# Top-k attention followed by an FNet block on one core: another order for seven matrix products over two PSUM banks, and another bank for the tail transposes of q and k

## The chip, the cores and the metric

The kernel runs on one core of a Trainium2 chip. The core has a matrix engine (TensorE, PE in the profile, with PEld for its weight loads), a vector engine (VectorE, DVE), a scalar engine (ScalarE, ACT), a general engine (GpSimd, POOL) and a queue engine (SyncE, SP) that here only issues transfers. Each engine works through its own list of instructions in order; semaphores hold an instruction until what it needs has been done on another engine. The metric is the device time of one execution in microseconds (us), lower is better. Everything is computed in float32.

## The reference, cut to what matters

```python
# q, k, v: (8 batches, 8 heads, 576 tokens, 64)
scores = q @ k.T / 8                                # per batch and head: 576 x 576
kth    = 32nd largest of each row                   # top_k = 32
scores = where(scores >= kth, scores, -1e9)
attn   = softmax(scores)
x      = attn @ v                                   # heads joined: (8, 576, 512)

mixed  = real(fft(fft(x, axis=tokens), axis=channels))
u      = x + mixed
un     = (u - mean(u)) / sqrt(var(u) + 1e-6)        # over the 512 channels
out    = u + relu(un @ w_ch1) @ w_ch2               # 512 -> 2048 -> 512
```

So every batch goes through attention with a top-k mask, through a Fourier transform over tokens and channels, and through a two-layer network (MLP).

## The kernel before, in words

**Attention.** The 64 heads are taken as 32 pairs. A pair has nine tiles of 128 query rows, four for each head and one that holds the 64 last rows of both. That gives 288 tiles, and the main loop takes one step for each, 36 steps for a batch. For a tile, `scores` (L355) multiplies on PE into PSUM and ACT copies the result to SBUF (`S`, L396 to L425); `top_ops` (L428) finds the 32nd largest by four rounds of MAX8 (L446) and MATCH_REPLACE8 (L448) on DVE; `bounds` (L451) makes the threshold on POOL; `mask` (L466) takes an ACT pass (L469) and a POOL pass (L472); `expo` (L476) is the exponential on ACT (L480); `plane` (L487) splits the result in two 16-bit halves on ACT (L493), which SP stores and transposes by DMA; some tiles are transposed on PE instead. `attend` (L576) multiplies by v on PE (L585), `attended` (L594) copies on ACT, and `to_tokens` (L615) transposes back on PE (`tpx`, L626) for DVE to normalise into x (L630).

`prep` (L309) transposes q and k of the next pair. It does so in two blocks for each of them: the four full 128-row blocks together (columns up to `NF` = 4), and then the tail block. For q the tail block is read from `qtail` and turned by a matrix of `turns` (L329), and ACT copies the result to qT (L337); for k, ACT copies the full blocks to kT (L339) and the tail in two pieces to `kt_t` (L343). `prep("q", pair + 1)` is issued at the first step of each pair (i % 9 = 0), right behind that step's scores, `prep("k", ...)` at the sixth.

**Fourier transform.** For a batch that is complete, folds of x (L671 to L770, on POOL, for the last batch on DVE) use the symmetry of the transform, then PE multiplies by the token tables (`yp`, L809) and the channel tables (`mp`, L860, L864), POOL adds the result to x (L898), DVE takes the statistics, and PE transposes to channels-first (`tpu`, L948).

**MLP.** `mlp_units` (L1041) puts the MLP of a batch into a queue of small units of PE work, in two halves of tokens: `ch` 0 with token tiles 0, 1 and the tail tile 4, `ch` 1 with tiles 2 and 3. `hidden` makes 16 blocks of the first layer (`hp`, L1055, read by ACT at L1059). The second layer is either `back` (`cp`, L1082 and L1120), or, for two token tiles at a time, `fast` (L1155): a Strassen-like scheme in which seven products of half size take the place of eight. It is used for `ch` 0 from the second batch on and for `ch` 1 of the last two batches, nine times in all. The units are handed out one after another by the main loop, a certain amount of PE time for each step (`some`, `level`), so that the MLP of one batch runs between the attention steps of the next. Other work has fixed places in this plan, given by `at(step, place, function)`.

**The seven products.** Each product (L1254) has two parts of eight matmuls 128x256, which are two units. The result goes to half of a PSUM bank, called `v`, `w` and, in the last batch, `z`; where a later product adds to what lies there, the bank keeps it in place:

| product | bank, half | weights | then |
|---|---|---|---|
| p2 | v lo | w2_21 | ACT reads it to a buffer `ct` (L1225), an adder adds that to x (L1227) |
| p5 | v hi | `w2_12` (T1) | the same; issues the load of T2 into `w2_12` |
| p1 | w lo | w2 itself | the same; half sums "11" and "12" (L1198) |
| p4 | w hi (z hi in the last batch) | `second` (T4) | the same; issues the load of T3; half sum "22" |
| p6 | w lo | `w2_12` (T2) | the same; issues the load of B12 |
| p3 | v hi | w2 itself | DVE adds the half bank to one half of x (L1211), v comes free |
| p7 | w lo | `second` (T3) | DVE adds the half bank to both halves of x (L1211), w comes free |

Products that add to what is in a half bank come after ACT has read it. The half sums of hidden values ("21", then "11", "12", "22") are made by POOL, after the last attention step by DVE; "11" is needed by p6, "12" by p3, "22" by p7, "21" by p5. In the last batch all seven results go to x by DVE (L1211), without the buffer. With p3 and p7 the finished token tiles are stored (`store_rows`, L1023): tiles 0 and 2 by a plain transfer from SP (L1028), the others by an indirect one from POOL (L1031).

**PSUM.** There are eight banks: two for scores (`ps_s`, tag "sp"), two for transposes (`ps_t`, tag "tp"), one for attention outputs, and three common ones that `bank()` (L144) hands out in turn. A caller that passes `hold=True` takes a bank out of the turn until it gives it back: `fast` does so with v, w and z, `back` with `cp`. All others (`hp` and most of the Fourier products) take the next one in the turn. In `tp` buffers there are q's and k's transposes (`tpq`, `tpk`), the transposed score tiles of `scores` (`sp_t`) and the other transposes.

```python
banks_free = [0, 1, 2]
def bank(shape, name, hold=False):
    n = banks_free.pop(0)
    t = ps_m.tile(shape, F32, name=name, tag=f"m{n}", bufs=1)
    if not hold:
        banks_free.append(n)
        return t
    return t, lambda: banks_free.append(n)
```

Of the kernel before, what the change touches and what calls it, by code (L numbers as in the profile page):

```python
# [9 lines left out]
F32 = mybir.dt.float32  # L10
# [9 lines left out]
P = 128  # L20
# [66 lines left out]
def kernel(  # L87
# [16 lines left out]
    NF = NC - 1  # L104
# [4 lines left out]
    NPB = H // 2  # L109
# [26 lines left out]
    ps_t = ctx.enter_context(tc.tile_pool(name="ps_t", bufs=2, space=bass.MemoryType.PSUM))  # L136
# [7 lines left out]
# [7 lines that stand above are left out]
# [158 lines left out]
    def prep(n, pair, blocks=((0, NF), (NF, NC))):  # L309

        if pair >= NPAIR:
            return 0.0
        src, got_of = nat[n, pair], qT_of if n == "q" else kT_of
        if pair not in got_of:
            got_of[pair] = attp.tile(
                [P, S if n == "q" else NF * P], F32, name=f"{n}T_{pair}", tag=f"{n}T",
                bufs=2 if n == "q" else 1
            )
        t_sb = got_of[pair]
        for c0, c1 in blocks:  # L320
            tp = ps_t.tile([P, 4, P], F32, name=f"tp{n}_{pair}_{c0}", tag="tp")
            for c in range(c0, c1):
                block, turn_by = src[:, c, :, :], ident
                if n == "q":
                    turn_by = turns[:, 2 if c == NF else c % 2, :]
                    if c == NF:
                        hp = pair % NPB
                        block = qtail[:, 2 * hp:2 * hp + 2, :]
                nc.tensor.transpose(  # L329
                    tp[:, c - c0, :], block.rearrange("p h d -> p (h d)"), turn_by  # L330
                )
            if c0 < NF:
                dst, got = t_sb[:, c0 * P:c1 * P], tp.rearrange("p a c -> p (a c)")[:, 0:(c1 - c0) * P]
            else:
                dst, got = t_sb[:, NF * P:], tp[:, 0, 0:TAIL]
            if n == "q":
                nc.scalar.mul(out=dst, in_=got, mul=scale)  # L337
            elif c0 < NF:
                nc.scalar.copy(out=dst, in_=got)  # L339
            else:  # L340
                for e in range(2):
                    r = slice(D * e, D * (e + 1))
                    nc.scalar.copy(out=kt_t[r, TAIL * e:TAIL * (e + 1)], in_=tp[r, 0, 0:TAIL])  # L343
        return 0.7
# [696 lines left out]
    def mlp_units(b):  # L1041
        x = x_of[b]
        last = b == B - 1
# [111 lines left out]
        def fast(ch):  # L1155
# [164 lines left out]
            def begin():  # L1320
# [6 lines left out]
                (0.0, lambda: mix("21", "21", "22", ALU.add), "back")  # L1327
            ] + [
                (1.75, lambda f=f, part=part: f(part), "back")
                for f in (p2, p5, p1, p4, p6, *((p7, p3) if last and ch else (p3, p7)))  # L1330
                for part in range(2)
            ]

# [1 line left out]
        for ch in range(2):  # L1335
            units += [
                (8 * CW[ch] / 1200.0, lambda ch=ch, it=it: hidden(ch, it), ("hidden", b, ch))
                for it in range(NIT)
            ]
            seven = b and ch == 0 or b >= B - 2  # L1340
            if seven:
                begin, products = fast(ch)
                if ch == 0:
                    begins.append(begin)
                else:
                    units.insert(1 - NIT, (0.0, begin, ("hidden", b, 1)))
                mix_first = products.pop(0)
                units.append(mix_first)
            for t in [t for t in CHUNKS[ch] if t == 4 or not seven]:
                units += [  # L1350
                    (1.75, lambda ch=ch, t=t, p=p: back(ch, t, p), "back")
                    for p in range(4 if t == 4 else 8)
                ]
            if seven:
                units += products
# [28 lines left out]
    for t in v_t:  # L1384
        nc.gpsimd.memset(t[TAIL:P, 0, NF, :], 0.0)
        nc.gpsimd.memset(t[0:TAIL, 1, NF, :], 0.0)
    nc.gpsimd.memset(ftail, 0.0)
    prep("q", 0, ((0, 2),))
    prep("k", 0)
    for c in range(2):  # L1390
        scores(0, c)
    prep("q", 0, ((2, NF), (NF, NC)))
    scores(2, 0)

# [88 lines left out]
    for b in range(B):  # L1483
        end = PER_BATCH * (b + 1) - 1
        last = b == B - 1
# [54 lines left out]
    def chunk_at(i):  # L1540

        for tile in (i - 5, i - 4, i - 3, i - 2):
            r = tile % PER_PAIR
            if PER_BATCH <= tile < N and r in (4, 8):
                if i - tile == ((5 if r == 4 else 4) if by_dma(tile) else 2 if tile in (2 * PER_BATCH - 1, N - 1) else 3):
                    return tile // PER_PAIR, r // 8
        return None, None
# [41 lines left out]
    while i < N + 5 or plan or queue or sums:  # L1589
# [37 lines left out]
        if pending and pending[0][0] <= i and (  # L1627
            i < 2 * PER_BATCH + 4 or chunk_at(i)[0] is None
        ):
            _, pp, pc = pending[0]  # L1630
# [12 lines left out]
        if short:  # L1643
            fixed += tok
            pair, r = divmod(i - 1, PER_PAIR)
# [40 lines left out]
        pair, ch = chunk_at(i)  # L1686
# [81 lines left out]
```

## Time and profile before

| | |
|---|---|
| median of 3 runs | 1778.69 us (1776.69 to 1779.95) |
| the profiled execution | 1780.27 us, its span 1778.5 us |
| busy in the span: PE, DVE, ACT, POOL | 1632.1, 1552.5, 1278.8, 906.6 us |
| mean granted clock of PE | 0.964 |
| chain that ended last, by engine | PE 48%, DVE 16%, ACT 16%, POOL 14%, issue 5%, DMA 2% |
| the products, L1254 (`cw`) | 512 matmuls, 383 ns each; idle before them 9.1 us, 6.2 of it to ACT's read L1225 |
| the products, L1254 (`cv`) | 432 matmuls, 383 ns each; idle before them 6.6 us |
| `hp`, L1055 | 2048 matmuls, 409 ns each; idle before them 6.8 us |
| q's tail transposes (`tpq` from `qtail`) | 32, 9.9 us with 273 ns as the median; idle before them 9.5 us, 9.2 of it to ACT's copy L396 |

The span is the time from the first to the last instruction in the profile. "Busy" is time in which an engine works on something; "idle before" is the time in which the engine stood just before an instruction of that group, with the event that ended it. PE is not busy for some 146 us of the span, and much of that lies in the first two batches, where weights are loaded and converted: in the page's forty slices PE has 5 to 7 tenths in the first five, and 8 or 9 in nearly all that follow. DVE has 9 tenths from the start to about 1600 us and little behind that, when the attention is finished and only the last MLPs remain.

### The profile page before, as it was taken

To read this page: it belongs to the slowest core of one execution; us is meant where nothing else is said; L and a number is where in the kernel's file an instruction comes from. 1 tells how busy PE (TensorE), PEld (TensorE's weight loads), DVE (VectorE), ACT (ScalarE), POOL (GpSimd) and SP (SyncE) were. 2 spreads that over 40 slices of the span, in tenths; PEclk is the share of its full clock that TensorE was granted. 3 is DMA by queue.
4 is the path that set the end of the run, shared out by engine and by line. 5 is a ranking of instruction groups with operands and counts; after the bars stand their busy time and mean duration, and the time that the engine had idled before them with its cause. 6 is when DMAs were issued, how large, how long until landed. Compare 5 with 4: busy or idle time off the path is not lost.

```text
span 1778.5 us, 26295 instructions
## 1 busy us (share of the span) xinstructions
PE 1632.1 (92%) x7830; PEld 1040.9 (59%) x7830; DVE 1552.5 (87%) x3319; ACT 1278.8 (72%) x3136; POOL 906.6 (51%) x1268
## 2 busy tenths in 40 slices
PE   5666689999898989999999999999999999999998
PEld 3444455464455755566555755576566755577777
DVE  7999989999999999998999999999999999863121
ACT  6888759887787878876888778877978787653200
POOL 4768846655634565354544665356535564333000
PEclk7778799999999999999999999999999999999999
DMA  5333126651457855586557856595558655643151
GB/s 156 115 102 117 32 81 163 185 152 50 119 145 196 222 131 135 136 233 161 135 136 200 212 133 140 152 240 145 152 132 222 182 135 128 172 114 101 36 180 60
DMA packets 492926, 255.28 MB, mean 144 GB/s; under 512 B 364528, under 2 KB 483056, under 8 KB 492784
## 3 DMA queue, kind: packets, MB, share of 16 engines
q1 hardware_dynamic: 489008, 243.80, 52.5%
q0 software_dynamic: 2816, 9.44, 1.6%
q8 instruction: 63, 1.03, 0.2%
q14 instruction: 79, 0.65, 0.1%
q10 hardware_dynamic: 960, 0.36, 0.1%
HBM read 99.79 MB, written 84.74 MB: 104 GB/s over the span
## 4 chain that ended last, share of the span: by engine, by line
PE 48%; DVE 16%; ACT 16%; POOL 14%; issue 5%; DMA 2%; POOLq 0%; SPq 0%; DVEq 0%; ACTq 0%
PE hp L1055 18%; DVE m L446 7%; DVE wk L448 6%; PE o L585 6%; PE cw L1254 5%; POOL wk L472 5%; PE cv L1254 4%; PE sp L422 4%; ACT wk L469 3%; POOL fold L696 3%; PE cp L1120 2%; ACT wk L493 2%; PE cp L1082 2%; ACT S L425 2%; PE sp_t L392 1%
## 5 line engine op out<-in xcount | busy, mean ns | idle before, releaser
L472 POOL TENSOR_TENSOR wk<-S,wk 128x576 f32<-128x576 f32 x288 | 407.6, 1415 | 418.1 <-ACT wk L469 417.2
L446 DVE MAX8 m<-wk 128x8 f32<-128x576 f32 x864 | 617.4, 741 | 0.1
L1055 PE MATMUL hp<-unT,w 128*128 128x256 f32 (+1 forms) x2048 | 529.6, 409 | 6.8 <-ACT hT L1059 6.0
L1055 PEld LDWEIGHTS hp<-unT,w 128*128 128x128 f32 x2048 | 378.0, 191 | 112.0 <-ACT hT L1059 11.4
L448 DVE MATCH_REPLACE8 wk<-m,wk 128x576 f32<-128x576 f32 x576 | 424.8, 737 | 0.0
L469 ACT ACTIVATE wk<-S,nt 128x576 f32<-128x576 f32 x288 | 224.3, 779 | 96.8 <-POOL nt L455 96.3
L493 ACT COPY wk<-S 128x576 uint16<-128x576 uint16 x468 | 290.2, 673 | 0.0
L446 DVE MAX8 m<-S 128x8 f32<-128x576 f32 x288 | 214.5, 745 | 11.6 <-ACT S L396 11.6
L480 ACT ACTIVATE S<-wk,nt 128x576 f32<-128x576 f32 x234 | 185.1, 791 | 46.7 <-POOL wk L472 45.4
L448 DVE MATCH_REPLACE8 wk<-m,S 128x576 f32<-128x576 f32 x288 | 212.5, 738 | 0.0
L1082 PE MATMUL cp<-w,hT 128*128 128x512 f32 x448 | 206.0, 598 | 0.0
L1059 ACT ACTIVATE hT<-hp 128x320 f32<-128x320 f32 (+1 forms) x256 | 104.1, 411 | 140.7 <-PE hp L1055 139.7
L585 PE MATMUL o<-PT,v 128*64 128x256 f32 (+3 forms) x1440 | 196.1, 417 | 5.6 <-DVE wk L448 2.1
L422 PE MATMUL sp<-kT,qT 64*128 64x512 f32 (+1 forms) x528 | 160.1, 668 | 6.7 <-ACT S L414 3.6
L585 PEld LDWEIGHTS o<-PT,v 128*64 128x64 f32 x1440 | 113.2, 154 | 84.1 <-issue 24.8
L425 ACT COPY S<-sp 128x512 f32<-128x512 f32 (+1 forms) x264 | 141.7, 589 | 26.2 <-PE sp L422 25.2
L455 POOL TENSOR_TENSOR nt<-m,cc 128x2 f32<-128x2 f32 x288 | 58.7, 204 | 166.9 <-DVE m L446 160.4
L1254 PE MATMUL cw<-w,hT 128*128 128x256 f32 x512 | 119.7, 383 | 9.1 <-ACT ct L1225 6.2
L1082 PEld LDWEIGHTS cp<-w,hT 128*128 128x128 f32 x448 | 81.3, 193 | 75.1 <-issue 74.7
L392 PEld LDWEIGHTS sp_t<-kt,qT 128*128 128x128 f32 x320 | 51.7, 195 | 111.4 <-issue 73.3
L1254 PEld LDWEIGHTS cw<-w,hT 128*128 128x128 f32 x512 | 94.5, 190 | 27.3 <-ACT ct L1225 8.4
L1254 PE MATMUL cv<-w,hT 128*128 128x256 f32 x432 | 100.4, 383 | 6.6 <-DMA w<-w_parts 2.8
(155 smaller groups left out, 2036.3 us busy)
## 6 DMA issues: line engine op xcount, KB each, us to landing
planes<-wk SPq DMA_DIRECT2D x208, 288.0 KB, 2.7
w<-w_parts SPq DMA_DIRECT2D x94, 512.0 KB, 4.7
space<-in_moe_w_ch_dram SPq DMA_DIRECT2D x32, 512.0 KB, 3.6
nat<-in_q_dram SPq DMA_DIRECT2D x128, 64.0 KB, 2.3
v<-in_v_dram SPq DMA_DIRECT2D x32, 256.0 KB, 3.4
nat<-in_k_dram SPq DMA_DIRECT2D x62, 128.0 KB, 2.8
planes<-wk SPq DMA_DIRECT2D x52, 144.0 KB, 2.7
w_parts<-w_t POOLq DMA_DIRECT2D x8, 512.0 KB, 4.0
```

The source lines that it names most:

```text
L422: nc.tensor.matmul(sp[r], lhsT=qT[hd, q_cols], rhs=kT[hd, :], start=True, stop=True)
L425: nc.scalar.copy(out=s_t[r, keys], in_=sp[r])
L446: ops.append(lambda src=src, m8=m8: nc.vector.max(out=m8, in_=src))
L448: ops.append(lambda src=src, m8=m8: nc.vector.match_replace(w, m8, src, NEG))
L469: nc.scalar.activation(out=w, in_=Ssb[i], func=AF.Relu, scale=-FAR, bias=Nt[i][:, 1:2])
L472: nc.gpsimd.tensor_tensor(out=w, in0=Ssb[i], in1=w, op=ALU.subtract)
L480: nc.scalar.activation(out=Ssb[i] if by_dma(i) else w, in_=w, func=AF.Exp, bias=Nt.pop(i)[:, 0:1], accum_out=den_t[pair % 3][:, c:c + 1],)
L493: nc.scalar.copy(out=words[:, half, :], in_=src[:, half, :])
L585: nc.tensor.matmul(o[D * e:D * (e + 1), c0:c1], lhsT=vv[:, e, c, :], rhs=pt[:, NF if c == NF else (NF + 1) * e + c, c0:c1], start=(c == 0) ...
L1055: nc.tensor.matmul(hp[:, 0:w], lhsT=w1[:, dt, P * it:P * (it + 1)], rhs=unT[:, dt, 0:w], start=(dt == 0), stop=(dt == NDT - 1),)
L1082: nc.tensor.matmul(cp, lhsT=hT[:, it, P * n:P * (n + 1)], rhs=w2[:, it, :], start=(it == 0), stop=(it == NIT - 1),)
L1254: nc.tensor.matmul(dst, lhsT=h()[a][:, kc, :], rhs=rhs_of(kc), start=start and kc == 0, stop=kc == NK - 1, skip_group_check=True,)
```

## The change

Two places differ.

1. The order in which `fast` puts its seven products into the queue. Before: p2, p5, p1, p4, p6, p3, p7, with p7 ahead of p3 in the second half of the last batch. By bank that is v v w w w v w. After: p2, p1, p5, p4, p3, p6, p7, by bank v w v w v w w; in both halves of the last batch p2, p1, p5, p4, p6, p3, p7, by bank v w v z w v w. The products are the same, and each carries its own loads, half sums and additions with it.

2. Where `prep` transposes the tail blocks. Before, they took a `tp` buffer always. After, those of the pairs 5 to 31 take a common bank from `bank()`, without holding it. The condition names the block and the pair, not q or k, and both have a block that starts at `NF`: so 27 of q's 32 tail blocks and 27 of k's change place.

```diff
@@ prep
         for c0, c1 in blocks:
-            tp = ps_t.tile([P, 4, P], F32, name=f"tp{n}_{pair}_{c0}", tag="tp")
+            shape, name = [P, 4, P], f"tp{n}_{pair}_{c0}"
+            if c0 == NF and pair > NPB:
+                tp = bank(shape, name)
+            else:
+                tp = ps_t.tile(shape, F32, name=name, tag="tp")
             for c in range(c0, c1):
@@ fast
                 (1.75, lambda f=f, part=part: f(part), "back")
-                for f in (p2, p5, p1, p4, p6, *((p7, p3) if last and ch else (p3, p7)))
+                for f in (p2, p1, p5, p4, *((p6, p3, p7) if last else (p3, p6, p7)))
                 for part in range(2)
             ]
```

## The prediction

> **What bounds the kernel now.** I read the page first, then the table of stretches, then one period of TensorE (PE) in order of time, then VectorE's (DVE) waits, then the end.
>
> ```profile
> span 1778.5 us, 26295 instructions
> PE 1632.1 (92%) x7830; PEld 1040.9 (59%) x7830; DVE 1552.5 (87%) x3319; ACT 1278.8 (72%) x3136; POOL 906.6 (51%) x1268
> ```
> ```profile
> 1173.00:1366.50 193.50, 190.15 (x920) 118.84 (x920) 185.62 (x399) 155.07 (x380) 103.89 (x153) 1.00 0.66 169
> 1721.00:1779.00 58.00, 52.58 (x242) 45.31 (x240) 9.39 (x16) 6.13 (x16) 1.92 (x2) 1.00 0.25 84
> ```
>
> Columns: length, then busy time of PE, weight load, DVE, ScalarE (ACT), GpSimd (POOL), granted clock, DMA. The first stretch is one period of the loop, from a stall of one batch's products to the same stall of the next: PE idles 3.35 us in it, DVE 7.9. Both are almost full, PE more so. After about 1600 us DVE has little left and PE alone sets the end.
>
> PE in the period, and one DVE row:
>
> ```profile
> 1161.58 3.69 PE L1254 MATMUL cv<-w,hT 128*128 128x256 f32 x16 [0.28 <-issue]
> 1168.89 3.62 PE L1254 MATMUL cw<-w,hT 128*128 128x256 f32 x16
> 1173.08 3.72 PE L1254 MATMUL cw<-w,hT 128*128 128x256 f32 x16 [0.56 <-ACT ct L1225]
> 1193.47 1.99 PE L1055 MATMUL hp<-unT,w 128*128 128x256 f32 x8 [0.56 <-ACT hT L1059]
> 1195.94 1.99 PE L1055 MATMUL hp<-unT,w 128*128 128x256 f32 x8 [0.47 <-ACT hT L1059]
> 1245.40 0.33 PE L329 MATMUL tpq<-turns,qtail 128*128 128x128 f32 x1 [0.54 <-ACT S L396]
> ```
> ```profile
> 1179.63 0.42 DVE L630 TENSOR_TENSOR x<-tpx,rd 128x256 f32<-128x256 f32 x1 [3.14 <-PE tpx L626]
> ```
>
> To see: the brackets are idle time and what ended it. p5 writes bank v just after p2 filled it and waits for ACT to read p2; p4 does the same to p1 in bank w. DVE then stands 3.14 us for a transpose (tpx) queued on PE behind these products. The two `hp` rows wait because v and w are still held and one bank serves all `hp`. q's tail block waits for the second `tp` buffer.
>
> The chain of waits at the end:
>
> ```profile
> 1752.34 0.03 issue
> 1752.36 0.49 DVE x L1211
> 1752.86 0.04 issue
> 1752.90 3.72 PE cv L1254 x16
> ...
> 1767.02 0.49 DVE x L1211
> ```
>
> **The change part by part.** A product that follows its bank-mate costs 0.56 us of waiting, and its sixteen matmuls take 3.72 instead of 3.45 us: 0.83 in all. (Restart after a wait: about 0.25, taken for every wait below.)
>
> *Order of the products, inside the loop.* The new order p2 p1 p5 p4 p3 p6 p7 has v w v w v w w, so one pair, p6-p7, is left. In sums of PE time:
> - Batch 1: gone are waits of 2.79 (p5 for its weights by DMA), 1.61 and 0.28, 5.4 with restarts. New: q's tail now takes the bank that DVE frees with L1140 and L1142, at 563.6 and later, about 1.0 us of waiting; and p6-p7. Net 2.9.
> - Batches 2 and 3: waits of 0.61, 0.56, 0.39 go, 2.3 with restarts. Batches 4 and 5: 0.28, 0.56 and 0.1 around tpk, 1.4.
> - Both kinds: v is freed one product earlier, so the second `hp` has a bank of its own; the two `hp` waits go, 1.5.
> - New in batches 1 to 5: p7 waits for ACT's read of p6. That read stands in ACT's queue behind L469, two L493 and an L480 that itself waits for POOL's L472. Moving the rows of 1181 to 1188 by the 1.5 us gained up to there, p6 ends at 1184.5 and ACT reads it at 1185.9 to 1186.4: a wait of 1.9, 2.2 with restart. Bounds: 0.56 (read at once) to 4.8 (one whole step of DVE). I take 1.9, as it comes from the rows themselves. Net for batches 2 and 3: 1.5 each; for 4 and 5: 0.7 each.
> - Batch 6, first half: 0.79, 2.33 and 0.61 go, 4.5 with restarts; p6-p7 have transposes between them, which leave about 1: net 3.0.
>
> Together 2.9 + 3.0 + 1.4 + 3.0 = 10.3.
>
> What else moves: the half sums (L1198, 1.28 us each) go ahead of the additions to x (L1227) and of the indirect store on POOL, because p1 is a product earlier. POOL's L472, due at 1168.04, comes some 0.35 later; the following ones come earlier with PE. Cover: ACT's chain at that place idles 0.99 us for the bound. On SyncE the loads of p5's and p4's successors move with their products; what is queued behind them, planes and their transposes, is issued 0 to 1.6 us earlier except where it stands behind p6's load (0 to 0.6 later). DVE needs those planes 1.4 us after they land now. I cost both at nothing; if that cover is gone, DVE stands by up to 0.6 per batch.
>
> *The tails in a common bank.* The condition names no q: k's tail block moves as well, 27 of each. For q, waits of 1.76 and 2.96 (batches 1 and 2), then four of about 0.53, go, 8 with restarts. Behind the 2.96, though, PE waits 1.77 for POOL's fold at 664.98, and behind the 1.76 it waits for other fold results: I take 0.5 and 1.2 of them, and 0.7 for each of the four, 4.5. For k there is nothing to gain (0.6 us of idle before all its transposes, ended by L551). Against that each tail takes a turn in the rotation of three banks. Its bank is read within 0.6 + 2 x 0.21 = 1.0 us (L339, then two L343; for q one read), and comes round again two `hp` or 3.8 us later; between the products, where one bank is left, nobody else asks for it until `hp` at 1191. So I take 0 for it. Bounds: 8, and minus 54 reads of 0.41 us (L1059), all uncovered, 22: minus 14.
>
> *The end.* Batch 6's second half has two such pairs, 1.65 us. But p3 now stands before `yp` and needs a half sum that DVE does after both outputs of the fold (L762). Counting DVE from its transpose, 2.85 us earlier than now, that sum ends at 1632.8 while PE could use it at 1630.8; `yp` starts at 1634.85 against 1634.58. Nothing gained, 0.3 lost. Batch 7: 0.83 once in its first half and twice in its second, 2.5 gained. Last operation:
>
> ```profile
> 1771.32 0.75 DVE L1211 SCALAR_TENSOR_TENSOR x<-cw,gi,x 128x512 f32<-128x512 f32 x1 [3.81 <-PE cw L1254]
> 1772.35 0.96 POOL L1031 DMA_INDIRECT out_dram<-x,out_list  x1 [49.08 <-DVE x L1211]
> 1774.77 0.48 DVE L1211 SCALAR_TENSOR_TENSOR x<-cv,gi,x 128x256 f32<-128x256 f32 x1 [2.70 <-PE cv L1254]
> 1775.29 0.34 SPq L1028 DMA_DIRECT2D out_dram<-x  x1
> ```
>
> The first pair (p7) now comes last: +0.27 on DVE, +0.24 to the issue (0.28 against 0.04), landing 2.7 (this one) against about 2.4 (1775.29 to the drain at 1777.7): 0.8 lost. Landings of indirect stores in this stretch reach 5.5; bounds 0.5 and 3.6. The Trainium skill, DMA: Bandwidth & Descriptors, Specifications, gives the first byte about 1 us from GpSimd and 0.6 from a hardware queue; by it the landing would differ by 0.4 instead of 0.3, and the sum by 0.1. p6's weights in batch 7 have one product less of time: issued 2.0 after p5 starts, landing 4.8, needed at 6.9. They fit by 0.1; I take 0, bounds 0 and 1.0. End: 2.5 - 0.3 - 0.8 = 1.4 gained.
>
> *Sum.* Loop 10.3 + 4.5 = 14.8, of which I let half reach the end: in a period DVE can follow PE only where it waits for it (3.14 + 0.97 + 0.58 + 0.78 = 5.5 of its 7.9 us), and folds on POOL and ACT's order hold the rest. Bounds 0 and all. 7.4 + 1.4 = 8.8. The profiled execution took 1780.27 (span 1778.5 and 1.77 around it), 1.58 over the median of 1778.69; against its own time 1771.5, against the median 1769.9. Forecast 1770.
>
> **The rivals.**
> 1. *Hidden anyway*, chance 0.18: DVE needs 185.6 of a period of 193.5 and fold chains set its start, so PE's gain in the loop turns into waiting and only the end's 1.4 counts: 1777.3. For it: DVE at 96%. Against: 41.2 us of DVE idle between 300 and 1600 name tpx on PE. The Trainium skill has such a case (TensorE: Matmul & The Clock Gate, HAM oscillation: PSUM double-buffering added no further gain, 126.6 to 125.5 us); the 0.56 waits above say that this kernel does stand for its banks.
> 2. *Slower*, chance 0.20: p7's wait for ACT's read of p6. It decides above 1.9 + 0.7 = 2.6 us in batches 4 and 5. At a whole step, 4.8, five batches lose 14.5 more: 1769.9 + 14.5 = 1784.4. For it: L480 waits for POOL, L472 idles 417 us for ACT, and all this stands on the order of in-order engines. Against: the rows moved give 1.9.
> 3. *Clock*, chance 0.02: more banks in turn, shorter and more frequent stops, and the granted clock drops from 1.00 to 0.99 over 1000 us: 10 us, 1780. The page named above has a section on it (A second HAM failure mode); here waits of 0.5 us at a clock of 1.00 speak against it.
>
> **How the numbers follow.** Forecast (part or all of the loop's gain arrives) 0.60. Range: all of the sum, 16.2, gives 1762.5; with the bounds of tails and landing 1761. Upwards it takes in rival 1, most of rival 2, and the tails' lower bound as far as 1783 (minus 14 in place of 4.5, half of it arriving: 1779.2). The forecast's own range is 1762 to 1775. This kernel's runs differ by 0.18%, so 0.2% (3.6 us) is what can be told from no change. Faster 0.64 (the forecast, and rival 1 where some gain arrives), same 0.15, slower 0.21.
>
> **What would show it.** Right: no wait of `cw` on L1225 between p1 and p4; tpx's 3.14 falls to about 1.6; the `hp` waits of 0.56 and 0.47 and the tail's 0.54 are gone; the period is 191 to 192.5; the end's chain has no DVE piece between products, and closes with an indirect store. Wrong: p7 waits over 2.6 us for L1225; DVE's wait for tpx stays while PE idles elsewhere; p3 of batch 6 stands for DVE by much more than 2; a wait of 1 us for `w_parts` in batch 7; a later landing of the last store.

## The result

The changed kernel takes 1785.95 us (median of 6 runs, 1784.26 to 1787.86) against 1779.32 us before (6 runs, 1776.69 to 1780.29): a ratio of 1.0040 with a 95% interval of 1.0027 to 1.0053. It is slower by 0.4%, and lies outside the predicted 1761 to 1783.

The page of the profile after, its span and its line of busy times:

```profile
span 1785.9 us, 26293 instructions
PE 1632.0 (91%) x7830; PEld 1048.9 (59%) x7830; DVE 1551.5 (87%) x3319; ACT 1280.8 (72%) x3136; POOL 909.3 (51%) x1268
```

The engines do the same work in the same time as before. What was added is standing. Lines of the changed kernel lie four further down than before (`hp` is L1059, the products L1258, DVE's addition from `cp` L1100).

One period of the loop, from one batch's stall of p7 to the next, in the table of stretches (length, busy PE, weight load, DVE, ACT, POOL, granted clock, DMA):

```profile
1194.00:1388.80 194.80, 189.00 (x921) 119.36 (x921) 185.69 (x399) 155.41 (x378) 104.03 (x153) 1.00 0.65 167
```

The period took 193.50 before and should have become 191 to 192.5; it is 1.3 longer, with DVE's work the same and PE idle for 5.8 us in place of 3.35.

PE in order of time at the products of this batch (start, length, instruction, and in brackets the idle time before it and what ended it):

```profile
1168.40 3.62 PE L1258 MATMUL cw<-w,hT 128*128 128x256 f32 x16
...
1175.89 3.62 PE L1258 MATMUL cv<-w,hT 128*128 128x256 f32 x16
1179.34 3.62 PE L1258 MATMUL cw<-w,hT 128*128 128x256 f32 x16
...
1188.50 3.62 PE L1258 MATMUL cw<-w,hT 128*128 128x256 f32 x16
1193.94 3.69 PE L1258 MATMUL cw<-w,hT 128*128 128x256 f32 x16 [1.82 <-issue]
...
1198.95 4.27 PE L1059 MATMUL hp<-unT,w 128*128 128x256 f32 x19
```

What the reader sees is what the new order was to do: p1, p5 and p4 follow one another without a wait, the two waits of `hp` behind the products are gone, and one wait is new, p7's for its bank-mate p6. ACT read p6's half bank from 1193.39 to 1193.84, behind four of its other instructions; the bracket names only "issue".

The new standing is elsewhere. PE's waits in the whole span (total, times, longest):

```profile
PE hp L1059 <- DVE x L1100: 12.9, 5, 3.1
...
PE cw L1258 <- issue: 8.0, 6, 1.8
PE o L589 <- DMA PT<-planes: 6.7, 3, 2.8
```

The first and the third of these rows do not exist before; the third is taken up further down. One of the five places, PE and then DVE, after the change:

```profile
1098.02 2.32 PE L1059 MATMUL hp<-unT,w 128*128 128x320 f32 x8
...
1100.61 0.27 PE L333 MATMUL tpq<-turns,qtail 128*128 128x128 f32 x1
...
1102.50 0.74 DVE L1100 SCALAR_TENSOR_TENSOR x<-cp,gi,x 128x512 f32<-128x512 f32 x1
...
1103.30 4.00 PE L1059 MATMUL hp<-unT,w 128*128 128x320 f32 x8 [2.42 <-DVE x L1100]
```

And the same place before:

```profile
1094.33 2.32 PE L1055 MATMUL hp<-unT,w 128*128 128x320 f32 x8
...
1096.92 0.27 PE L329 MATMUL tpq<-turns,qtail 128*128 128x128 f32 x1
1097.03 2.32 PE L1055 MATMUL hp<-unT,w 128*128 128x320 f32 x8
...
1097.93 0.74 DVE L1096 SCALAR_TENSOR_TENSOR x<-cp,gi,x 128x512 f32<-128x512 f32 x1
...
1102.71 2.42 PE L1055 MATMUL hp<-unT,w 128*128 128x320 f32 x8
```

Of the three common banks one is held here by `cp_3`, the result of token tile 3, until DVE has added it to x. That addition is put off to the end of DVE's next step (`late_next`, L1105 of the kernel before). Two banks are left for the first two blocks of `hp`, and the third block, 5.7 us later, finds `cp_3`'s bank free. After the change q's tail takes the second bank, so the second `hp` is the one that has to wait for DVE. On DVE the addition stands behind a whole step of MAX8 and MATCH_REPLACE8.

### The profile page after: what moved, and what is told of

Same layout as the page of the kernel before. It is cut to its first block, busy times and chain, and to the rows that moved or that the text cites. A ratio compares the mean times of both kernels' runs of the same rounds, so it can differ in the third digit from the quotient of the medians.

```text
span 1785.9 us, 26293 instructions
## 1 busy us (share of the span) xinstructions
PE 1632.0 (91%) x7830; PEld 1048.9 (59%) x7830; DVE 1551.5 (87%) x3319; ACT 1280.8 (72%) x3136; POOL 909.3 (51%) x1268
## 4 chain that ended last, share of the span: by engine, by line
PE 55%; DVE 15%; ACT 12%; POOL 11%; issue 4%; DMA 3%; SPq 0%; POOLq 0%; DVEq 0%; ACTq 0%
PE hp L1059 21%; PE o L589 7%; DVE m L450 6%; DVE wk L452 6%; PE cw L1258 5%; PE cv L1258 5%; PE sp L426 4%; POOL wk L476 4%; PE cp L1124 3%; POOL fold L700 3%; ACT wk L473 3%; PE sp_t L396 2%; PE cp L1086 2%; PE tpP L552 1%; DMA planes<-wk 1%
## 5 line engine op out<-in xcount | busy, mean ns | idle before, releaser
L1059 PE MATMUL hp<-unT,w 128*128 128x256 f32 (+1 forms) x2048 | 532.7, 412 | 19.7 <-DVE x L1100 12.9
L1059 PEld LDWEIGHTS hp<-unT,w 128*128 128x128 f32 x2048 | 381.4, 192 | 124.8 <-DVE x L1100 14.0
L1258 PE MATMUL cw<-w,hT 128*128 128x256 f32 x512 | 118.5, 381 | 8.3 <-issue 8.0
L1258 PEld LDWEIGHTS cw<-w,hT 128*128 128x128 f32 x512 | 95.0, 190 | 24.1 <-issue 11.6
L1258 PE MATMUL cv<-w,hT 128*128 128x256 f32 x432 | 101.0, 383 | 1.9 <-DVE hT L1202 1.9
```

The costliest lines, as they stand in the source:

```text
L1059: nc.tensor.matmul(hp[:, 0:w], lhsT=w1[:, dt, P * it:P * (it + 1)], rhs=unT[:, dt, 0:w], start=(dt == 0), stop=(dt == NDT - 1),)
L1258: nc.tensor.matmul(dst, lhsT=h()[a][:, kc, :], rhs=rhs_of(kc), start=start and kc == 0, stop=kc == NK - 1, skip_group_check=True,)
```

## The experiments

The theory was that this one turn of the tail costs the time (A). Against it stood: the new order costs it (B), both cost some (C), and later, every tail's turn costs a little (D). Besides medians, single profiles are compared in stretches: the time between the first MAX8 of one tile and that of another.

**1. The order alone.** Tails stay in `tp`.

```diff
-for f in (p2, p5, p1, p4, p6, *((p7, p3) if last and ch else (p3, p7)))
+for f in (p2, p1, p5, p4, *((p6, p3, p7) if last else (p3, p6, p7)))
```

> Only the new order of the seven products; all tails stay in tp buffers. Theory A (the tails' turn in the common banks costs the time: hp stands 12.9 us in five places for the bank of cp_3, which DVE frees late): no wait of hp for DVE's addition from cp is left, and the order by itself gains or is even, 1773 to 1779 us. Rival B (the order costs the time: p7 stands 1.74 to 1.83 us behind p6 in four batches, 8.0 us in all, and attention stands 6.7 us for planes that SP issues later): about as slow as the whole change, 1783 to 1787, with both waits still there. Rival C (each part costs some): 1780 to 1783.

Measured: 1774.92 us (12 runs, 1772.07 to 1781.32) against 1779.2; ratio 0.9977 (0.9964 to 0.9989). The order makes the kernel faster, by 4.1 us, though p7's waits are all there (again 8.0 us in six places, longest 1.8). B is out, and C with it: the order by itself costs nothing.

**2. The tails alone.** Old order, q's and k's tails of pairs 5 to 31 in a common bank.

```diff
-            tp = ps_t.tile([P, 4, P], F32, name=f"tp{n}_{pair}_{c0}", tag="tp")
+            shape, name = [P, 4, P], f"tp{n}_{pair}_{c0}"
+            if c0 == NF and pair > NPB:
+                tp = bank(shape, name)
+            else:
+                tp = ps_t.tile(shape, F32, name=name, tag="tp")
```

> Only the tails of q and k in a common bank; the products in the old order. Theory A: hp waits for DVE's addition from cp about 2.3 to 3.1 us in five places, and the time is 1784 to 1792. Rival B: 1774 to 1780, less than before by the tail's own waits of up to 8 us. Rival C: 1780 to 1784.

Measured: 1789.71 us (1786.48 to 1791.96) against 1779.2; ratio 1.0047 (1.0033 to 1.0061). The waits are there again, in a kernel whose products are in the old order:

```profile
PE hp L1059 <- DVE x L1100: 12.2, 5, 2.7
```

**3. Only q's tails in a common bank.** Old order; k's stay in `tp`.

```diff
-            if c0 == NF and pair > NPB:
+            if n == "q" and c0 == NF and pair > NPB:
```

> Old order of the products; only q's tails in a common bank, k's stay in the tp buffers. Theory A holds that it is q's tail that takes the turn between two hp at the place where cp_3 is held: same time as with both tails moved, within 2 us, and the same five waits of hp. If k's tails cost or gain by themselves, the two differ by more than 2 us.

Measured: 1792.79 us (1787.48 to 1794.18); ratio 1.0068 (1.0055 to 1.0081), five waits of 12.8 us in all. So q's tails carry the loss. The medians of experiments 2 and 3 differ by 3.1 us, more than the 2 us expected; that k's tails would win something back still cannot be read from it, as the intervals of 1.0068 and 1.0047 overlap.

**4. p4-p6 in one bank instead of p6-p7.** Tails in `tp`.

```diff
-for f in (p2, p5, p1, p4, p6, *((p7, p3) if last and ch else (p3, p7)))
+for f in (p2, p1, p5, p4, p6, p3, p7)
```

> Order p2 p1 p5 p4 p6 p3 p7 everywhere, tails in tp buffers. The pair in one bank is now p4-p6 in place of p6-p7 (the last batch is as in the whole change, with z). Theory A and B alike: the wait of 1.8 us of cw before p7 goes; before p6 there comes a wait for ACT's read of p4, 0.6 us if ACT reads at once, up to 1.8 if the read stands in ACT's queue. If 0.6, the time is under that of the order alone by up to 6 us (five batches of 1.2); if DVE bounds the period anyway, the two are within 2 us.

Measured: 1771.8 us (1770.63 to 1775.05); ratio 0.9950 (0.9937 to 0.9962), the better of the two orders by 0.27%. p7 no longer waits; in its place p6 waits in some batches for its weights (`w_parts`): they are loaded into the place that p5 has read from, and p6 now comes one product earlier than before behind that load's issue:

```profile
PE cw L1254 <- DMA w<-w_parts: 6.3, 4, 2.1
```

Why this order is the better one stays open: the waits are of much the same size, 6.3 us here and 8.0 us in experiment 1. In single profiles the end is 186.4 us long in place of 189.2.

**5. All of the change but the one tail.** New order, all tails moved except q's of the fourth pair of a batch.

```diff
-            if c0 == NF and pair > NPB:
+            if c0 == NF and pair > NPB and not (n == "q" and pair % NPB == 3):
```

> The whole change, but q's tail of the fourth pair of each batch (pair % 4 == 3), the one that takes its turn while cp_3 is held, stays in tp; 20 of q's tails and 27 of k's still move. Theory A (that one turn costs the time): the five waits of hp for DVE's addition are gone, about the order alone (1775) or up to 4 us under it: 1770 to 1777. Rival D (every tail's turn costs a little): 47 of 54 turns are left, so 1783 to 1786.

Measured: 1775.52 us (12 runs, 1771.25 to 1778.46) against 1780.57; ratio 0.9968 (0.9958 to 0.9979). Of the waits 0.2 us are left:

```profile
PE hp L1059 <- DVE x L1100: 0.2, 1, 0.2
```

47 of the 54 moved tails cost nothing that can be seen, and gain nothing either: the order alone had 0.9977. D is out. The profiles show why nothing is gained: the waits change places. With the order alone q's transposes wait 10.5 us for ACT's copy `S` and `hp` 1.3 us for ACT's reads. Here the 10.5 are 0.5, but q's tail now has to wait where its common bank still holds a Fourier result that ACT has yet to read (`yt`) or the tail tile's result that DVE has yet to read (`ct`, 1.0 us), and `hp` waits longer for ACT's reads:

```profile
PE hp L1059 <- ACT hT L1063: 6.2, 5, 2.9
...
PE tpq L333 <- ACT yt L851: 4.2, 1, 4.2
```

**6. Only that one tail.** Old order, seven q tails (pairs 7, 11, ... 31) in a common bank.

```diff
-            if c0 == NF and pair > NPB:
+            if n == "q" and c0 == NF and pair > NPB and pair % NPB == 3:
```

> The old order, and only those seven q tails (pairs 7, 11, ... 31) in a common bank, nothing else changed. Theory A: five waits of 2.2 to 3.3 us of hp for DVE's addition, and a time near that of all tails moved: 1787 to 1793. Rival D: 7 of 54 turns, 1779 to 1781.

Measured: 1787.99 us (1785.18 to 1790.28) against 1780.57; ratio 1.0045 (1.0030 to 1.0059), as much as with all 54.

```profile
PE hp L1059 <- DVE x L1100: 9.9, 5, 3.3
```

Only the longest of the five waits is as long as expected; the other four are 1.5 to 1.9 us, under the 2.2 expected, and the loss comes all the same (see "Half of PE's gain" below). Taken away the loss goes, put in alone it comes: A is shown from both sides.

**7. The bank freed earlier.** The whole change, but DVE's addition from `cp_3` is issued at once.

```diff
-                    if last:
-                        finish()
-                    elif t == 3:
-                        late_next.append(finish)
+                    if last or t == 3:
+                        finish()
```

> The whole change, but DVE's addition from cp_3 is not put off to the end of the next step; it is issued where the other tiles' results are read, one step of DVE earlier, so the bank is free when hp asks. Theory A: hp's waits for the addition fall from 12.9 to under 3 us in all, 1771 to 1778. If the tails cost by something else than the held bank, the time stays at 1783 to 1787.

Measured: 1808.61 us (1805.31 to 1809.73) against 1780.57; ratio 1.0158 (1.0141 to 1.0174). The waits of `hp` for the addition are gone, as expected, and the time is far worse, which was not:

```profile
DVE x L1100 <- PE cp L1086: 29.4, 6, 6.6
```

DVE now meets the addition before PE has finished `cp_3`, stands 29.4 us for it in six places, and everything behind it on DVE is late. `hp` waits all the same, now for ACT's `unT` (22.0 us in six places). The late addition protects DVE; the bank it holds is its price. What A says of the held bank is not touched; what it expected of this kernel was wrong.

**8. The better order and the harmless tails.** Order of experiment 4, tails of experiment 5.

> Order p2 p1 p5 p4 p6 p3 p7 everywhere (1771.8 with all tails in tp) and the tails in common banks except q's of each fourth pair. Theory A: no wait of hp for the addition, and what the other tails waited for tp (q's tails behind S, 10.8 us in eight places, much of it hidden) may come back: 1767 to 1772, the fastest so far. Rival D: 1776 to 1782.

Measured: 1772.58 us (1770.50 to 1775.70) against 1780.57; ratio 0.9955 (0.9941 to 0.9970), just above the expected 1767 to 1772 and the same as with all tails in `tp` (0.9950). The moved tails are worth nothing here either.

**9 and 10. The end alone, and the loop alone.** Tails in `tp`. In 9 the new order is used in batch 6's second half and in batch 7; in 10 in the first halves of batches 1 to 6.

```diff
-for f in (p2, p5, p1, p4, p6, *((p7, p3) if last and ch else (p3, p7)))
+# 9
+for f in ((p2, p1, p5, p4, *((p6, p3, p7) if last else (p3, p6, p7))) if ch or last
+          else (p2, p5, p1, p4, p6, p3, p7))
+# 10
+for f in ((p2, p1, p5, p4, p3, p6, p7) if not (ch or last)
+          else (p2, p5, p1, p4, p6, *((p7, p3) if last and ch else (p3, p7))))
```

> Old order in the loop (first halves of batches 1 to 6), new order only where it ends: second half of batch 6 and both halves of batch 7; tails in tp. If the new order loses at the end by p3 of batch 6 standing 1.92 us for DVE's half sum and gains nothing by the rest, as the stretches behind the last attention step say (189.2 us against 187.8): 1.4 us slower than before, 1780 to 1782, and the stretch again 189.2. If the prediction's 1.4 us of gain at the end holds, 1777 to 1778.

> New order only in the loop (first halves of batches 1 to 6), the old one for the second half of batch 6 and for batch 7; tails in tp. With the end's loss left out: 1.4 us under the order alone, some 1773.5 (1772 to 1775), with the stretch behind the last attention step at 187.8 us. If the end gained as predicted, 1776 to 1777.

Measured: the end alone 1780.81 us against 1780.48, ratio 1.0002 (0.9994 to 1.0011); the loop alone 1773.85 us, ratio 0.9963 (0.9949 to 0.9977). All of the order's gain is in the loop. The predicted gain of 1.4 us at the end (a ratio of 0.9992) lies just outside the interval; the loss of 1.4 us that single profiles suggested (1.0008) lies inside it and is neither shown nor excluded. In the profile of experiment 9, its fastest execution, p3 of batch 6 stood 1.93 us for DVE's half sum too, but the stretch behind the last tile was 187.7 us, as before (see the last section).

**11. p6 first only where it looked better.** Tails in `tp`.

```diff
-for f in (p2, p5, p1, p4, p6, *((p7, p3) if last and ch else (p3, p7)))
+for f in (p2, p1, p5, p4, *((p6, p3, p7) if last or ch or b == 1 else (p3, p6, p7)))
```

> Tails in tp; p6, p3, p7 close the products in batch 1, in the second half of batch 6 and in batch 7, p3, p6, p7 in the first halves of batches 2 to 6. If the stretches of single profiles add up (tiles 72 to 108: 198.3 us with p6 first against 200.7; tiles 279 to 287: 51.7 with p3 first against 53.4; behind the last attention step: 186.4 against 189.2), it lies 1 to 3 us under the order with p6 first everywhere: 1769 to 1771 against 1771.8, at least as fast as every other. If they do not, 1772 to 1775.

Measured: 1771.83 us (1770.53 to 1775.00) against 1782.42; ratio 0.9943 (0.9928 to 0.9959), against 0.9950 in experiment 4. The intervals overlap widely, so these runs cannot tell level from the hoped-for 1 to 3 us. In its own profile the three stretches came out much as hoped (198.6, 51.7 and 187.2 us), but its span, 1773.2 us, is that of experiment 4, 1773.3: what the stretches gained was lost in others. Both kernels are 0.5% to 0.6% faster than the kernel before and 0.9% to 1.0% faster than the changed one.

The stretches of the single profiles, in us (tiles 72 to 108 hold batch 1's products, 252 to 279 one of the five places, 279 to 287 the products of batch 6's first half, the last column what follows the last tile):

| kernel | 72-108 | 252-279 | 279-287 | 287 to end |
|---|---|---|---|---|
| before | 197.5 | 150.4 | 57.2 | 187.8 |
| whole change | 200.2 | 154.0 | 51.7 | 189.5 |
| 1 order | 200.7 | 150.4 | 51.7 | 189.2 |
| 2 tails | 200.3 | 153.6 | 57.2 | 187.8 |
| 3 q's tails | 197.1 | 153.6 | 58.8 | 187.8 |
| 4 p6, p3, p7 | 198.3 | 150.5 | 53.4 | 186.4 |
| 5 not the fourth | 203.2 | 150.8 | 51.7 | 189.1 |
| 6 only the fourth | 199.1 | 153.5 | 57.2 | 187.8 |
| 7 freed early | 202.0 | 160.9 | 51.7 | 189.6 |
| 8 p6 first, not the fourth | 198.2 | 150.3 | 53.4 | 186.5 |
| 9 end only | 197.5 | 150.5 | 57.2 | 187.7 |
| 10 loop only | 203.8 | 150.6 | 51.7 | 187.8 |
| 11 mixed | 198.6 | 151.5 | 51.7 | 187.2 |

The second column splits by q's fourth tail: 150.3 to 151.5 without it, 153.5 to 154.0 with it, experiment 7 aside. The third splits by the order: 57.2 or more with the old one, 51.7 with p3 first, 53.4 with p6 first. The first column scatters: experiments 1 and 10 have the same code there and 200.7 and 203.8 us. Stretches in between differ by 2 to 4 us between profiles of the same code there, and are not used.

## Why the prediction was wrong, step by step

**The tails: this step failed.** The prediction said that a tail's bank "comes round again two `hp` or 3.8 us later", and took 0 for the turns in the rotation and 4.5 us of gain. It reckoned with v and w being held, but not with `cp_3`, which stays held until DVE's postponed addition. The runs show five waits of 2.3 to 3.1 us, and +0.47% (8 us) in place of the 2.25 us of gain that it let reach the end. Even its lower bound, 54 reads of 0.41 us, was the wrong price: not one ACT read of 0.41 us but the rest of a DVE step. The rows of the profile before held the number. There the second `hp` starts at 1097.03, in the bank that the tail will take, and `cp_3`'s bank is free at 1097.93 + 0.74 = 1098.67: from these rows some 1.6 us of waiting, as an estimate. As for the 0.53 us waits of q's tails and the two longer ones that were to be gained: experiments 5 and 8 show no gain from taking them away. The prediction's 1.0 us for DVE's late read was right, but at one place the tail also stands 4.2 us for ACT's `yt`, which had no term, and `hp` stands 4.9 us more for ACT (experiment 5 against 1).

**The order in the loop: the size was right by luck.** Half of 10.3 us was predicted; the loop alone gains 0.37% (6.6 us, 4.1 to 9.1). But it did not come from where it was put, and two terms of the sum do not follow from their parts: batch 6's 4.5 less "about 1" is 3.5 and not 3.0, and batch 1's 2.9 gives p6-p7 no number. Batch 6's first half gave 5.4 us in the stretch of its products, where 3.0 were counted. Batch 1, where 2.9 were counted, gave none: the stretch 72 to 108 took 200 to 204 us where p3, p6, p7 close the products of batch 1, and 197 to 200 with the old order, tails moved or not. The prediction costed the planes' transposes on SP at nothing. They are not late by the clock: SP issues the one in question at 575.56 to 577.98 in the profiles of the whole change and of experiments 1 and 10 and at 578.05 before. But PE, without its own waits for weights and for ACT, is at the attention product at 576 to 578 us instead of 584.75, and now stands there. Before:

```profile
584.75 2.38 PE L585 MATMUL o<-PT,v 128*64 128x256 f32 x20
```

From the profile of experiment 1:

```profile
572.10 3.62 PE L1254 MATMUL cv<-w,hT 128*128 128x256 f32 x16
...
580.62 4.53 PE L585 MATMUL o<-PT,v 128*64 128x256 f32 x20 [4.90 <-DMA PT<-planes]
```

That is rival 1, a wait that takes the place of another, true in one batch. Behind the wait the same twenty matmuls also take 4.53 us instead of 2.38 (the last section has more on this). In batches 2 to 5 no part could be told from the scatter.

**p7 behind p6: right.** 1.9 us was read from the rows of before, 1.74 to 1.83 was measured in batches 2 to 5, and 0.61 in batch 1. Rival 2, built on this wait, did not decide: below its 2.6 us, and experiment 1 gained with the wait in it.

**DVE's wait for tpx: right.** 3.14 us was to fall to about 1.6 and is 1.73 in that batch.

**The end: mostly right in its pieces, wrong in the sum.** The three waits of 0.58 us between products of batch 7 are gone. p6's weights there were late by 0.31 us (0 taken, 1.0 the bound). The last addition is the 512 wide one and is followed by an indirect store. p3 of batch 6 was said to stand by 2 us (1632.8 against 1630.8), and stood 1.92. The sum of 1.4 us of gain does not show: 1.0002 (0.9994 to 1.0011) for the end alone. The term of the last store was too small: from the start of the last product to the end of the span it is 7.4 us before and 9.5 us in experiment 9, so 2.1 us are lost where 0.8 were counted, most of it behind the issue of the indirect store. With it the sum is 2.5 - 0.3 - 2.1 = 0.1, as the stretch of experiment 9 has it (187.7 against 187.8). It also left out that the granted clock can fall behind p3's wait (last section).

**Half of PE's gain reaches the end.** For the loss this was too low: 12.2 us of waits cost 8.4 us in experiment 2, and 9.9 us cost 8.0 in experiment 6. The stretch 252 to 279 shows how. In experiment 6 `hp` waits 1.56 us there for DVE's addition, and the next block of `hp` 0.94 us more for ACT's read; from q's tail to the attention product behind them PE needs 7.55 us in place of 4.51. DVE needs a transpose that stands on PE behind all this, and waits longer by the same 3 us, which is also what the stretch lost. DVE's row before:

```profile
1502.60 0.42 DVE L630 TENSOR_TENSOR x<-tpx,rd 128x256 f32<-128x256 f32 x1 [2.55 <-PE tpx L626]
```

And in experiment 6:

```profile
1509.75 0.42 DVE L634 TENSOR_TENSOR x<-tpx,rd 128x256 f32<-128x256 f32 x1 [5.60 <-PE tpx L630]
```

DVE's other waits of 0.3 us or more in this stretch agree within 0.05 us. So here a delay of PE reaches the end whole, and not by half.

## What to carry to other kernels

Where buffers are handed out in turn, count the turns at the place where one of them is held, and ask who frees it and when: a read of 0.4 us can hide a release that stands behind a whole step of another engine. Here 47 extra turns cost nothing that could be seen and the turns at one place cost everything, so look at each place and do not multiply an average. Ask also what a removed wait will meet next: the 10 us that q's tails no longer waited for `tp` came back as waits for common banks. And a release that is put off may be put off for a reason: here freeing the bank earlier made the kernel 1.2% slower than holding it did (1.0158 against 1.0040).

## What the runs showed of the hardware

A stop of PE of about 1.9 us or more may cost more than its length: in some cases the granted clock of PE (1.00 is full speed) falls behind it. Windows of about 4 us behind two of the five stops of the changed kernel (length, busy PE, weight load, DVE, ACT, POOL, clock, DMA):

```profile
1103.30:1107.30 4.00, 4.00 (x10) 2.18 (x12) 4.00 (x9) 3.66 (x9) 1.86 (x3) 0.59 0.40 90
...
1300.00:1304.10 4.10, 4.10 (x22) 2.43 (x24) 4.10 (x10) 3.77 (x9) 1.86 (x3) 1.00 0.46 103
```

Behind the stop of 2.42 us the clock is 0.59, behind the one of 2.66 us it is 1.00. The eight `hp` matmuls took 4.00 us there and 2.42 here, so the first stop cost 1.6 us more than its length. It happened behind four of the five stops of the changed kernel, two of five with the tails alone, one of five with q's tails alone and two of five in experiment 6. The same accounts for the end in single profiles: behind p3's wait of 1.92 us the clock was 0.65 to 0.67 in the profiles of the changed kernel and of the order alone (stretches of 189.2 and 189.5 us), and 1.00 behind the 1.93 us of experiment 9 (187.7 us). From the matmuls behind p3's wait to the same Fourier product (`yp`) PE needed 6.42 us in the changed kernel and 4.84 in experiment 9. None of p7's waits of 1.74 to 1.83 us was followed by slower matmuls (3.69 us for sixteen). Rival 3 had the clock fall by many short stops; it fell behind few long ones. From 500 to 1000 us and from 1000 to 1500 us the mean clock is 0.98 and 0.99 in the profile of the changed kernel and 1.00 in both before, about the size that rival 3 named, so some of the loss of the whole change can be lost clock; how much was not separated. The clock is not the main cause of the tail's loss: the six executions of experiment 6 lose 8.0 us with mean clocks of 0.962 to 0.968, where the 17 of the kernel before beside them have 0.960 to 0.967. As an estimate, 8 us lost by the clock alone would be 16 us at 0.50, which lowers the mean over 1780 us by 0.004.

The Trainium skill, TensorE: Matmul & The Clock Gate, What's actually happening, has the clock at half after at least one idle window of about 3.4 us, which runs freely and does not start with the kernel's work. The trace agrees on the half, with 0.50 from 1104.3 to 1107.3 us, and stops of much the same length that end either way fit a window that runs freely. It differs on the length: stops of 1.92 to 3.10 us in the changed kernel and of 1.88 us in experiment 6 were enough.
